# Where the weights' low words are shifted, and for how long TensorE's pauses are filled

## The chip, the cores and the metric

The kernel runs on 1 core of one Trainium2 chip. Times are device microseconds (us); the figure for a kernel is the median of several runs. The engines: TensorE (PE) multiplies, from weights that it loads first (PEld), into PSUM, eight banks of 128 x 2 KB; VectorE (DVE) and ScalarE (ACT) read and write PSUM and SBUF; GpSimd (POOL) works on SBUF alone; SyncE (SP) issues the transfers. Each runs its own queue in order.

## The reference, cut to what matters

Attention, then two mixtures, over 4 x 576 = 2304 tokens of 512 features. q, k and v are float32; the first mixture's and the second's weights are float64, which the kernel receives as pairs of 32-bit words and has to turn into float32 itself.

```python
# attention, 8 heads of 64: pooled by 4 and repeated, plus a band of +-3
out_up = np.repeat(sm_attn(q_d, k_d, v_d), 4, axis=2)
scores = np.where(mask, scale * q @ k.T, -1e9)      # |i - j| < 4
x = out_up + softmax(scores) @ v
# first mixture: 512 -> 2048 -> 512
h = x @ w_in; x = (h * np.cos(h)) @ w_out
# second mixture: 512 -> 1536 -> 512
xn = x / rms * rms_g
out = (silu(xn @ w_gate) * (xn @ w_val)) @ w_out2
```

## The kernel before

Every large product is made of three float32r products (high x high, high x low, low x high). The first mixture goes in units: a `unit` makes a 128 x 512 block of h in one PSUM bank (`h`, L1004), ScalarE, VectorE and again ScalarE and VectorE turn it into h cos h (L1022 to L1029), it is split into high and low (L1038, L1040), and `second` multiplies it with w_out into the banks `y` (L1070). The first tokens' units start while the attention of the other three batches is still to be done; its blocks (`block`: transposes `btr`, scores `bs`, softmax L693 to L706, transposes `bat`, values `bav`) and its pooled part (`pq_part`, `pooled`: `trq`, `sps`, `tra`, `avp`) lie between the units. The second mixture (`gvp` L1493, `o` L1746) comes after, with Strassen-like sums.

The order of all engines' queues comes from a planner, the class `Order`. Every piece of work is a generator that yields its next step, as an engine with a price in us, or a list of alternatives. `start` works out for each when it could begin: the engine's clock `free`, and the end of the step before plus a handover (0.12 on the same engine, 0.3 between engines, 0.2 behind TensorE). Of alternatives it takes the one that ends first, with a handicap as a fifth entry. `run` always takes the step that can start first, ties and near ties by due times. The instructions are issued in that order; on the chip semaphores hold them, not the planner's times. Banks are handed out from a pool in planned time (`take("bank")`).

The conversion of a piece of weights, 128 x 512 float64 words, is `w_conv` (first mixture, 32 pieces) and `w2_conv` (second, 36 pieces, whose result goes back to DRAM). The float64 lies as pairs of int32, low word `lw` and high word `hw`. Its steps: the low word is shifted right by 29 on VectorE (L311, L1295); ScalarE scales the high word, read as float32, by a power of two (L315, L1297); VectorE joins `hw` shifted left by 3 with `lw` (L317, L1299). In the first mixture ScalarE then rounds to float32r (L319) and GpSimd or VectorE takes the difference (L322). The step `yield "ACT", 0.0` ahead of the shift makes it wait, in planned time, for ScalarE's turn.

`keep_warm` (L239) is called whenever TensorE gets a step, with the planned end of its last step and the planned start of this one. Up to the planner's `FT` = 90 it fills `FR` = 0.8 of the pause with float32 products of the 128 x 128 identity, reckoned at 0.22 us each, into a bank that is free at the pause's start (L246). They add nothing to the planner's clocks.

Of the kernel before, what the change touches and what calls it, by code (L numbers as in the profile page):

```python
# [9 lines left out]
F32 = mybir.dt.float32  # L10
F32R = mybir.dt.float32r
I32 = mybir.dt.int32
ACTF = mybir.ActivationFunctionType
ALU = mybir.AluOpType
AX = mybir.AxisListType
# [23 lines left out]
NCV = 5  # L39
FR = 0.8  # L40
FT = 90
SLACK = 2.5
CU = 4
DS = 0
# [2 lines left out]
TP = 5  # L47
WD = 0.005
NQS = 1
CVB, GLB = 9, 0.5  # L50
T0, T1, U1, U2 = 70, 52, 6.5, 4.26
DU = {"conv": 20, "pool": -320, "blk": -200}
# [2 lines left out]
class Order:  # L55
# [102 lines left out]
    def run(self):  # L158
        while self.parts:
            can = [(c, p) for p in self.parts for c in (self.start(p),) if c]  # L160
            assert can, [(p["gen"].__name__, p["req"]) for p in self.parts]
            (t, step), p = min(can, key=lambda x: x[0][0])
            kind = step[1] if step else p["req"][1]

            (t, step), p = min((x for x in can if x[0][0] <= t + self.NEAR and (x[0][1][1] if x[0][1] else x[1]["req"][1]) == kind),
                               key=lambda x: ((x[1]["due"] + (TP if TP and x[0][1] and x[0][1][4] else 0)) * WD + x[0][0], x[0][0]))
            r = p["req"]
            if step is None:
                val = None
                if t > p["t"]:  # L170
                    p["t"], p["eng"] = t, "?"
                if r[0] == "take":
                    have = self.pools[self.which(r)]
                    x = min(have, key=lambda x: x[0])
                    have.remove(x)
                    val = x[1]
            else:
                t, eng, dur, tab, sw = step
                if sw and TP is not None:
                    t += self.TABLE  # L180
                if tab:
                    self.table = tab
                if eng == "PE" and self.fill:
                    self.fill(self.free.get(eng, 0.0), t)
                self.free[eng] = t + dur
                p["t"], p["eng"] = t + dur, eng
                val = (t + dur, eng)
            self.next(p, val)
# [3 lines left out]
def fused_kernel(ctx: ExitStack, tc, q, k, v, w_in, w_out, w_gate, w_val, w_out2, rms_g, mask, bmask, out):  # L192
    nc = tc.nc
    PE, ACT, DVE, POOL, SP = nc.tensor, nc.scalar, nc.vector, nc.gpsimd, nc.sync
    S_ = Order()
# [27 lines left out]
    def bank_tile(i, shape, name):  # L223
        return psum.tile(shape, F32, tag=f"b{i}", name=name)


    ident = const.tile([128, 128], F32, name="ident")
# [7 lines left out]
    ident_r = const.tile([128, 128], F32R, name="ident_r")  # L235
    ACT.activation(out=ident_r, in_=ident, func=ACTF.Copy)

    def keep_warm(t0, t1):

        n = int((t1 - max(t0, 2.5)) * FR / 0.22)  # L240
        have = [x for x in S_.pools["bank"] if x[0] <= t0]
        if t0 > FT or n < 1 or not have:
            return
        t = bank_tile(have[0][1], [128, 128], "warm")
        for _ in range(n):
            PE.matmul(t, ident, ident, start=True, stop=True)  # L246

    S_.fill = keep_warm if FR else None
    ysc = dram.tile([NTILE, 2, 128, DM], F32, name="ysc")
# [44 lines left out]
    def conv_due(m, i):  # L294
        if m == 1:
            return T0 + (i // 4) * CU + (0.0, 5.0)[i % 2] + DU["conv"]
        return T0 + T1 * NTILE + (i // 3) * U2 + (0.0, 0.0, 4.0)[i % 3] + DU["conv"]

    def w_conv(m, i, raw, rp, r):
        if i:  # L300
            yield wait(("cv", m, i - 1))
        cv = yield take("cv")
        p = yield take("wa" if i < NF else "wb" if i < NF + NB else "wa" if i < 32 - NW else "wg")
        done(("cv", m, i), 0.0)
        w = p[1] if p[2] == "wg" else p[0].tile([128, 2, 512], F32R, tag=p[1], name="w" + p[1])
        raw = raw.rearrange("p (b c) -> p b c", c=2)
        hw, lw = raw[:, :, 1], raw[:, :, 0]
        c = hw.bitcast(F32)
        yield "ACT", 0.0
        a = yield "DVE", 0.34  # L310
        DVE.tensor_scalar(out=lw, in0=lw, scalar1=29, scalar2=None, op0=ALU.logical_shift_right)  # L311


        yield "ACT", 0.62
        ACT.activation(out=c, in_=c, func=ACTF.Prelu, scale=2.0 ** -112, alpha=-2.0 ** 32)  # L315
        yield "DVE", 0.7
        DVE.scalar_tensor_tensor(out=hw, in0=hw, scalar=3, in1=lw, op0=ALU.logical_shift_left, op1=ALU.bitwise_or)  # L317
        yield "ACT", 0.62
        ACT.activation(out=w[:, 0], in_=c, func=ACTF.Copy)  # L319
        give("cv", cv)  # L320
        _, e = yield [("POOL", 1.5), ("DVE", 0.8, None, None, CVB)]
        (POOL if e == "POOL" else DVE).tensor_tensor(out=w[:, 1], in0=c, in1=w[:, 0], op=ALU.subtract)  # L322
        give(rp[2], rp)
        give("raw", r)
        W[m, i], WP[m, i] = (w[:, 0], w[:, 1]), p
        done(("w", m, i))
# [298 lines left out]
    def block(b, u, raw, pools):  # L625

        i0, n, r0, off = geo(u)
# [7 lines left out]
        for w in range(2):  # L635
            yield take("att")
            i = yield take("bank")
            t = bank_tile(i, [128, 4, 128], "btr")
# [8 lines left out]
            _, e = yield [("ACT", 0.6), ("DVE", 0.68, None, None, 0.3)]  # L647
# [22 lines left out]
        held = []  # L670
        for e in range(2):
            yield take("att", 1 - e)
            i = yield take("bank")
            held.append((i, bank_tile(i, [128, 4, 64], "bs")))
        yield "PE", 1.0

        for _, t in held:
# [12 lines left out]
        t0 = (S_.cur["t"], "PE")  # L690
# [44 lines left out]
        for e in range(2):  # L735
            yield take("att", 1 - e)
            i = yield take("bank")
            held.append((i, bank_tile(i, [128, 4, 116], "bav")))
        yield "PE", 1.0
        v_i = VI[b, u]  # L740
        for a in range(4):
# [242 lines left out]
    def unit(n):  # L984
# [11 lines left out]
        h = bank_tile(i, [128, 512], "h")  # L996
        for ci, c in enumerate(cs):
            wh, wl = W[1, 2 * c]
            yield "PE", 1.44 if len(cs) > 1 else 2.76
            m = 0  # L1000
            for kk in range(4):
                ksl = slice(kk * 128, kk * 128 + 128)
                for a, x in ((wh, xh), (wh, xl), (wl, xh)):
                    PE.matmul(h[:, w_ * ci:w_ * ci + w_], a[:, ksl], x_at(x, kk), start=m == 0, stop=m == 11)  # L1004
                    m += 1
            if j == len(T1S) - 1:
                free_w(WP[1, 2 * c])
# [280 lines left out]
    def w2_conv(i, raw, p, r):  # L1288
        c, kind = divmod(i, 3)
        pairs = raw.rearrange("p (b c) -> p b c", c=2)  # L1290
        hw, lw = pairs[:, :, 1], pairs[:, :, 0]
        f = hw.bitcast(F32)
        yield "ACT", 0.0
        yield "DVE", 0.34
        DVE.tensor_scalar(out=lw, in0=lw, scalar1=29, scalar2=None, op0=ALU.logical_shift_right)  # L1295
        yield "ACT", 0.62
        ACT.activation(out=f, in_=f, func=ACTF.Prelu, scale=2.0 ** -112, alpha=-2.0 ** 32)  # L1297
        yield "DVE", 0.7
        DVE.scalar_tensor_tensor(out=raw[:, 0:512], in0=hw, scalar=3, in1=lw, op0=ALU.logical_shift_left, op1=ALU.bitwise_or)  # L1299
        yield "SP", 0.8  # L1300
        SP.dma_start(wfs[c, :, 512 * kind:512 * kind + 512], raw[:, 0:512].bitcast(F32))
        give(p[2], p, S_.now())
        give("raw", r, S_.now())
        count(("wfs", c), 3)
# [534 lines left out]
```

## Time and profile before

| | |
|---|---|
| median of 3 runs | 984.79 us (983.96 to 986.35) |
| profiled execution | 986.51 us |
| its span, first to last instruction | 984.7 us |
| mean granted TensorE clock | 0.994 |
| busy: TensorE, VectorE, ScalarE, GpSimd | 97%, 74%, 55%, 27% of the span |

The profile is of one execution. Busy shares are averages over stages with quite different limits; the tables by stage give busy time per engine in a stretch of the span, counted from its start. The granted clock (PEclk) is a share of full speed: 1.00 is 2.4 GHz, 0.50 is 1.2 GHz, and a value between is a stretch with both. In a timeline, the bracket at the end of a row is how long the engine was idle before it, and what ended that. A float32 filler product leaves two matmul records.

### The profile page before, as it was taken

What the parts mean: (1) busy time and instruction counts of PE and PEld (TensorE: products, weight loads), DVE (VectorE), ACT (ScalarE), POOL (GpSimd) and SP (SyncE); (2) the same over time, 40 slices, a digit from 0 to 9 for tenths busy, and PEclk for the clock granted to TensorE, in tenths of its full rate; (3) what the DMA queues carried; (4) which work ended last, traced back from release to release, by engine and by line L of the source; (5) the groups of instructions that cost most, each with busy time, mean ns of one, the idle gap of its engine ahead of it and who ended that gap; (6) DMA issues with size and microseconds to landing.
All of it is one profiled execution on the core that took longest, in us unless ns stands there. A gap on an engine that the chain in (4) does not pass through costs nothing.

```text
span 984.7 us, 19115 instructions
## 1 busy us (share of the span) xinstructions
PE 954.6 (97%) x7102; PEld 881.4 (90%) x7102; DVE 724.0 (74%) x1460; ACT 542.8 (55%) x1090; POOL 268.5 (27%) x325
## 2 busy tenths in 40 slices
PE   7788899999999999999999999999999999999998
PEld 7787788888988888888888889999999999999998
DVE  3889976577767675666577599586666688999895
ACT  3657886577676964657566475242322334544442
POOL 3867675444345311000042252000000014300000
PEclk9999999899999999999999999999999999999999
DMA  8788633567675554544331311133222144454432
GB/s 245 211 234 252 179 116 118 140 204 185 201 220 153 173 168 137 167 153 165 124 129 65 107 43 49 49 105 93 75 81 70 57 146 131 137 169 137 143 119 76
DMA packets 160333, 136.07 MB, mean 138 GB/s; under 512 B 72176, under 2 KB 133744, under 8 KB 160240
## 3 DMA queue, kind: packets, MB, share of 16 engines
q1 hardware_dynamic: 160240, 134.85, 45.4%
q8 instruction: 56, 0.92, 0.4%
q14 instruction: 37, 0.30, 0.1%
HBM read 98.64 MB, written 36.18 MB: 137 GB/s over the span
## 4 chain that ended last, share of the span: by engine, by line
PE 83%; POOL 4%; DVE 3%; SPq 3%; issue 3%; DMA 2%; ACT 2%; DVEq 0%; POOLq 0%; ACTq 0%
PE gvp L1493 26%; PE y L1070 19%; PE h L1004 18%; PE o L1746 13%; PE bav L745 2%; PE btr L641 1%; SPq L475 1%; POOL wwa L322 1%; DMA v<-in_v 1%; SPq L807 1%; PE avp L589 1%; PE bs L684 1%; PE yt L1398 1%; PE bat L720 1%; SPq L478 1%
## 5 line engine op out<-in xcount | busy, mean ns | idle before, releaser
L1493 PE MATMUL gvp<-xc,wc 128*128 128x384 f32 x1296 | 231.7, 335 | 0.0
L1493 PEld LDWEIGHTS gvp<-xc,wc 128*128 128x128 f32 x1296 | 225.6, 188 | 0.3
L1564 DVE TENSOR_TENSOR tmp<-gvp,tmp 128x384 f32<-128x384 f32 x180 | 99.3, 553 | 54.6 <-PE gvp L1493 51.4
L1004 PE MATMUL h<-big,wwa 128*128 128x256 f32 (+1 forms) x756 | 126.1, 320 | 1.6 <-DVE t L1029 1.0
L1004 PEld LDWEIGHTS h<-big,wwa 128*128 128x128 f32 x756 | 109.4, 193 | 11.9 <-DVE t L1029 1.2
L1746 PE MATMUL o<-wo,wc 128*128 128x256 f32 x972 | 118.9, 280 | 0.0
L1746 PEld LDWEIGHTS o<-wo,wc 128*128 128x128 f32 x972 | 116.1, 190 | 0.0
L1070 PE MATMUL y<-wwa,big 128*128 128x512 f32 x432 | 109.6, 398 | 1.7 <-DVE big L1040 1.7
L1070 PEld LDWEIGHTS y<-wwa,big 128*128 128x128 f32 x432 | 78.9, 188 | 18.7 <-DVE big L1040 2.7
L1004 PE MATMUL h<-big,wwb 128*128 128x256 f32 (+1 forms) x504 | 85.2, 320 | 0.1
L1070 PE MATMUL y<-wwb,big 128*128 128x512 f32 x324 | 82.3, 399 | 2.3 <-POOL big L1040 2.3
L1024 DVE SCALAR_TENSOR_TENSOR t<-kk,h 128x512 f32<-128x512 int32 x72 | 49.0, 681 | 42.4 <-ACT kk L1022 42.1
L1004 PEld LDWEIGHTS h<-big,wwb 128*128 128x128 f32 x504 | 73.1, 193 | 7.7 <-issue 0.8
L1022 ACT ACTIVATE kk<-h 128x512 int32<-128x512 f32 x72 | 42.7, 593 | 58.4 <-PE h L1004 58.2
L1070 PEld LDWEIGHTS y<-wwb,big 128*128 128x128 f32 x324 | 59.0, 188 | 14.7 <-POOL big L1040 2.9
L1630 POOL TENSOR_TENSOR wt<-wo 128x256 f32<-128x256 f32 x10 | 9.9, 987 | 208.7 <-DVE wc L1349 183.3
L1029 DVE TENSOR_TENSOR t<-h,t 128x512 f32<-128x512 f32 x72 | 49.3, 685 | 18.1 <-ACT t L1027 17.6
L1555 ACT ACTIVATE tmp<-gvp 128x384 f32<-128x384 f32 x36 | 17.7, 492 | 75.9 <-PE gvp L1493 75.9
L1027 ACT ACTIVATE t<-t,cst 128x512 f32<-128x512 f32 x72 | 51.9, 722 | 13.2 <-DVE t L1024 12.7
L1038 ACT ACTIVATE big<-t 128x512 fp32r<-128x512 f32 x72 | 45.2, 629 | 25.0 <-DVE t L1029 23.6
L1689 ACT ACTIVATE wc<-ut 128x512 fp32r<-128x512 f32 (+1 forms) x60 | 34.3, 584 | 43.4 <-DVE ut L1675 27.2
L1040 DVE TENSOR_TENSOR big<-t,big 128x512 fp32r<-128x512 f32 x54 | 40.0, 741 | 16.5 <-ACT big L1038 16.2
(185 smaller groups left out, 1737.8 us busy)
## 6 DMA issues: line engine op xcount, KB each, us to landing
us<-tmp SPq DMA_DIRECT2D x72, 192.0 KB, 2.0
uf<-us SPq DMA_DIRECT2D x48, 256.0 KB, 2.9
rawwa<-in_moe_w_out SPq DMA_DIRECT2D x21, 512.0 KB, 4.5
wfs<-rawwa SPq DMA_DIRECT2D x36, 256.0 KB, 2.3
rawwa<-in_moe_w_gate SPq DMA_DIRECT2D x12, 512.0 KB, 4.0
rawwa<-in_moe_w_val SPq DMA_DIRECT2D x12, 512.0 KB, 4.4
wf<-wfs SPq DMA_DIRECT2D x12, 512.0 KB, 4.1
vb<-in_v SPq DMA_DIRECT2D x80, 64.0 KB, 2.7
```

Of the source, the lines that this page charges most:

```text
L1004: PE.matmul(h[:, w_ * ci:w_ * ci + w_], a[:, ksl], x_at(x, kk), start=m == 0, stop=m == 11)
L1022: ACT.activation(out=kk, in_=h, func=ACTF.Copy, scale=INV2PI, bias=0.25)
L1024: DVE.scalar_tensor_tensor(out=t, in0=kk, scalar=TWOPI, in1=h, op0=ALU.mult, op1=ALU.subtract)
L1027: ACT.activation(out=t, in_=t, func=ACTF.Sin, scale=-1.0, bias=cst[:, 0:1])
L1029: DVE.tensor_tensor(out=t, in0=h, in1=t, op=ALU.mult)
L1038: ACT.activation(out=gh, in_=t, func=ACTF.Copy)
L1040: (POOL if e == "POOL" else DVE).tensor_tensor(out=gl, in0=t, in1=gh, op=ALU.subtract)
L1070: PE.matmul(y[j][b], g[:, tsl], a, start=(first and ci == 0 and i == 0), stop=(last and c == 15 and i == 2))
L1493: PE.matmul(bank, w[:, a, kk], xc[:, x, b, kk], start=first and i == 0, stop=i == 5, skip_group_check=True)
L1564: DVE.tensor_tensor(out=half(o), in0=a, in1=half(b), op=ALU.add)
L1689: ACT.activation(out=o[:, 0], in_=src, func=ACTF.Copy)
L1746: PE.matmul(b[m][1][:, l], u[0][x][:, j, l], w[:, y, k], start=(p == 0 and l == 0 and i == 0), stop=(p == C3 - 1 and i == 2), skip_group_c ...
```

## The change

The shift becomes a helper, `shift`, used by both conversions. It offers the step to VectorE and to ScalarE, each for 0.6 us (VectorE's price was 0.34), with a handicap `SHB` of 0 for ScalarE. On VectorE the instruction is the old one. On ScalarE an activation reads the upper 16 bits of the low word as unsigned 16-bit integers (every fourth of them), multiplies by 2^-13, adds 2^-14 - 0.5 and writes the result, rounded to an integer, over the low word.

`keep_warm` fills on beyond the planner's 90, until `FT2` = 215: there only pauses of 0.8 us and over, and 0.6 of them. If no bank is free at the pause's start, the products go into a bank that the waiting step itself holds and is about to overwrite, where the step has named one (`own`). The band's scores, the band's values and the units' h do.

```diff
+FT2, FR2 = 215, 0.6
+SHB = 0.0
...
-                    self.fill(self.free.get(eng, 0.0), t)
+                    self.fill(self.free.get(eng, 0.0), t, p)
...
-    def keep_warm(t0, t1):
-        n = int((t1 - max(t0, 2.5)) * FR / 0.22)
+    def keep_warm(t0, t1, p):
+        own = p.pop("own", None)
+        n = int((t1 - max(t0, 2.5)) * (FR if t0 < FT else FR2) / 0.22)
         have = [x for x in S_.pools["bank"] if x[0] <= t0]
-        if t0 > FT or n < 1 or not have:
+        if n < 1 or t0 > FT2 or t0 > FT and t1 - t0 < 0.8:
             return
-        t = bank_tile(have[0][1], [128, 128], "warm")
+        if have:
+            own = bank_tile(have[0][1], [128, 128], "warm")
+        elif t0 < FT or own is None:
+            return
         for _ in range(n):
-            PE.matmul(t, ident, ident, start=True, stop=True)
+            PE.matmul(own, ident, ident[:, :own.shape[-1]], start=True, stop=True, skip_group_check=True)
...
+    def shift(raw, lw):
+        _, e = yield [("DVE", 0.6), ("ACT", 0.6, None, None, SHB)]
+        if e == "ACT":
+            top = raw.bitcast(U16).rearrange("p (b c) -> p b c", c=4)[:, :, 1]
+            ACT.activation(out=lw, in_=top, func=ACTF.Copy, scale=2.0 ** -13, bias=2.0 ** -14 - 0.5)
+        else:
+            DVE.tensor_scalar(out=lw, in0=lw, scalar1=29, scalar2=None, op0=ALU.logical_shift_right)
...
         yield "ACT", 0.0
-        a = yield "DVE", 0.34
-        DVE.tensor_scalar(out=lw, in0=lw, scalar1=29, scalar2=None, op0=ALU.logical_shift_right)
+        yield from shift(raw2, lw)
         yield "ACT", 0.62
...
+        S_.cur["own"] = held[0][1][:, 0:2].rearrange("p a k -> p (a k)")
         yield "PE", 1.0
...
+        S_.cur["own"] = held[0][1][:, 0]
         yield "PE", 1.0
...
+            if ci == 0:
+                S_.cur["own"] = h[:, 0:128]
             yield "PE", 1.44 if len(cs) > 1 else 2.76
```

## Rows read from the trace of the kernel before

**Rows 1.** The page: busy time by engine (part 1); a group of instructions (part 5).

```profile
PE 954.6 (97%) x7102; PEld 881.4 (90%) x7102; DVE 724.0 (74%) x1460; ACT 542.8 (55%) x1090; POOL 268.5 (27%) x325
...
L1022 ACT ACTIVATE kk<-h 128x512 int32<-128x512 f32 x72 | 42.7, 593 | 58.4 <-PE h L1004 58.2
```

**Rows 2.** Busy us by stretch: length, PE, PEld, DVE, ACT, POOL, PEclk, DMA, GB/s.

```profile
70.00:130.00 60.00, 53.92 (x456) 46.63 (x455) 56.90 (x95) 49.48 (x95) 40.75 (x43) 0.97 0.71 204
100.00:160.00 60.00, 55.24 (x431) 48.30 (x430) 50.92 (x99) 51.87 (x105) 42.34 (x49) 0.97 0.48 142
20.00:200.00 180.00, 160.00 (x1557) 142.36 (x1557) 140.70 (x260) 128.00 (x272) 119.60 (x142) 0.97 0.64 182
70.00:200.00 130.00, 119.73 (x1012) 105.59 (x1011) 99.84 (x175) 95.98 (x183) 80.89 (x91) 0.96 0.57 165
200.00:450.00 250.00, 248.34 (x2168) 216.87 (x2167) 170.55 (x331) 169.37 (x315) 74.06 (x100) 1.00 0.60 177
```

**Rows 3.** TensorE's timeline: start, us, instruction, count [idle before <- what ended it].

```profile
96.40 1.42 PE L1070 MATMUL y<-wwa,big 128*128 128x512 f32 x5 [1.17 <-DVE big L1040]
...
106.16 1.54 PE L534 MATMUL sps<-pqs 64*72 64x144 f32 x8 [2.66 <-DVE bst L704]
...
138.12 1.43 PE L1070 MATMUL y<-wwb,big 128*128 128x512 f32 x5 [1.09 <-POOL big L1040]
...
169.28 0.32 PE L745 MATMUL bav<-bt,vb 64*64 64x58 f32 x2 [0.15 <-ACT pqs L396]
171.25 1.96 PE L745 MATMUL bav<-bt,vb 64*64 64x58 f32 x30 [1.64 <-DVE bt L755]
...
187.29 3.14 PE L1004 MATMUL h<-big,wwa 128*128 128x256 f32 x24 [1.01 <-DVE t L1029]
```

**Rows 4.** Busy time by stretch, around the two stretches of lowered clock.

```profile
100.00:110.00 10.00, 7.34 (x50) 6.68 (x49) 9.90 (x19) 9.23 (x14) 5.64 (x7) 0.83 0.87 247
106.00:110.00 4.00, 3.84 (x20) 3.44 (x21) 4.00 (x9) 3.93 (x6) 1.75 (x3) 0.57 0.81 224
170.00:178.00 8.00, 6.75 (x53) 6.62 (x54) 3.80 (x6) 2.85 (x6) 6.79 (x10) 0.57 0.50 107
```

**Rows 5.** Busy time by stretch of L311 alone, the first mixture's shift.

```profile
20.00:200.00 180.00, 21.84 (x32) 0.97 0.64 182
70.00:130.00 60.00, 11.80 (x15) 0.97 0.71 204
100.00:160.00 60.00, 7.73 (x12) 0.97 0.48 142
```

**Rows 6.** Line L311: ns min/median/max, first and last start.

```profile
L311 DVE TENSOR_SCALAR rawwa<-rawwa x18: 376/594/1210, 83.3 to 180.5; 128x512 int32<-128x512 int32 x18
L311 DVE TENSOR_SCALAR rawwb<-rawwb x14: 379/426/1544, 30.7 to 85.3; 128x512 int32<-128x512 int32 x14
```

**Rows 7.** Line L315, the scaling of the high word: ns min/median/max.

```profile
L315 ACT ACTIVATE rawwb<-rawwb x14: 659/676/744, 28.7 to 86.0; 128x512 f32<-128x512 f32 x14
```

**Rows 8.** ScalarE's timeline, 95 to 105 us.

```profile
97.88 1.24 ACT L315 ACTIVATE rawwa<-rawwa 128x512 f32<-128x512 f32 x2
```

**Rows 9.** VectorE's timeline, 96 to 107 us.

```profile
97.46 1.20 DVE L311 TENSOR_SCALAR rawwa<-rawwa 128x512 int32<-128x512 int32 x1
...
99.25 0.88 DVE L311 TENSOR_SCALAR rawwa<-rawwa 128x512 int32<-128x512 int32 x1
...
103.67 1.02 DVE L311 TENSOR_SCALAR rawwa<-rawwa 128x512 int32<-128x512 int32 x1
104.62 1.26 DVE L703 TENSOR_SCALAR bst<-bst 128x8 f32<-128x8 f32 x1
105.91 0.20 DVE L704 RECIPROCAL bst<-bst 128x8 f32<-128x8 f32 x1
```

**Rows 10.** Busy time by stretch of L1295 alone, the second mixture's shift.

```profile
190.00:450.00 260.00, 18.14 (x36) 1.00 0.59 175
```

**Rows 11.** The chain that ended last, 70 to 80 us: start, us, what.

```profile
76.44 0.89 PE warm L246 x8
...
77.48 1.66 PE h L1004 x12
```

More of the change, by code (lines that the diff above doesn't have):

```diff
@@ L12 @@
 I32 = mybir.dt.int32
+U16 = mybir.dt.uint16
 ACTF = mybir.ActivationFunctionType
@@ L305, in w_conv @@
         w = p[1] if p[2] == "wg" else p[0].tile([128, 2, 512], F32R, tag=p[1], name="w" + p[1])
+        raw2 = raw
         raw = raw.rearrange("p (b c) -> p b c", c=2)
@@ L1293, in w2_conv @@
         yield "ACT", 0.0
-        yield "DVE", 0.34
-        DVE.tensor_scalar(out=lw, in0=lw, scalar1=29, scalar2=None, op0=ALU.logical_shift_right)
+        yield from shift(raw, lw)
         yield "ACT", 0.62
```

## The prediction

> **What bounds the kernel now.** I read the page's first part, then a table of busy time by stage, then TensorE's timeline for its waits, and last the stretches in which the clock is low. TensorE is busy 97% of the span [rows 1]. From 200 us on there is nothing to win: in 200 to 450 it is busy 248.34 of 250 us at granted clock 1.00 [rows 2]. What can move lies ahead of that. Between 70 and 200 us TensorE is idle 130 - 119.73 = 10.3 us [rows 2]. Five waits of over a microsecond make 1.17 + 2.66 + 1.09 + 1.64 + 1.01 = 7.6 us of it [rows 3]; VectorE ends four of them, 6.5 us, and GpSimd the one of 1.09.
>
> The clock falls behind two of these waits. Behind the one of 2.66 us it is granted at 0.57 over 4 us, behind the one of 1.64 us at 0.57 over 8 us [rows 4]. At the half level (1.2 instead of 2.4 GHz) a microsecond does half a microsecond's work, so 0.57 leaves 0.43 of the stretch undone: 4 x 0.43 = 1.7 us and 8 x 0.43 = 3.4 us, together 5.1 us. What can be won at all is thus 10.3 + 5.1 = 15.4 us, 1.6%.
>
> Of the helpers VectorE is the fullest first: 56.90 of 60 us in 70 to 130, ScalarE 49.48. In 100 to 160 they stand level, 50.92 and 51.87 [rows 2]. So ScalarE has far less room there than its 55% on the page [rows 1] suggests.
>
> **The change part by part.**
>
> *The shift leaves VectorE.* The first mixture has 32 conversions, and their shifts on VectorE take 21.84 us [rows 5], 0.68 each, from 0.38 to 1.54 [rows 6]. On ScalarE no row shows this operation. The nearest is the step behind it, which also reads and writes every second word of 128x512: 0.66 to 0.74 us [rows 7], and two in a row 1.24 [rows 8], so about 0.6 of the engine's time each. The lower bound is the 0.59 of the activation that writes int32, which reads PSUM [rows 1]; above, I allow for twice the row, 1.35, since the source is now every fourth 16-bit word. I take 0.6, by the neighbour step, which has the same partitions, count and output stride.
>
> How many move: both candidates bid 0.6 with no handicap, and the step is reached when ScalarE's turn comes (the step of zero length ahead of it). From there the planner lets ScalarE start 0.12 later and VectorE 0.3 later, so ScalarE wins unless its queue is over 0.18 us longer. I take about two thirds, 22 of 32 (bounds 10 and 32). In 20 to 200 us VectorE then loses 22 x 0.68 = 15 us and ScalarE gains 22 x 0.6 = 13 us: 140.70 becomes about 126, and 128.00 about 141, of 180 us [rows 2]. The sum hardly changes. But in 70 to 130, where VectorE is full, 15 shifts take 11.80 us [rows 5], and two thirds of these are 8 us of 60.
>
> What of it is on the path: ahead of the longest wait VectorE carries shifts of 1.20, 0.88 and 1.02 us in 97 to 105 us, and then a tiny operation of 1.26 us [rows 9]; the reciprocal behind it ends TensorE's wait of 2.66 us [rows 3]. Taking two of three shifts out gives back 2 us on VectorE, but ScalarE is itself busy 9.23 of 10 us there [rows 4] and takes 1.2 more, so about 0.8 is left for sure. Of the 6.5 us that VectorE ends I count a good third as won, 2.5 us (bounds: -1 if ScalarE hands everything back, 6.5 if all four go). Before 70 us I add 0.5 for shifts standing between steps of the attention blocks (bounds 0 and 2). What is late next is the ScalarE step between two products, the sines and exponentials.
>
> *Second mixture, 36 conversions.* Their shifts take 18.14 us on VectorE [rows 10]. TensorE idles 1.7 us in 200 to 450 [rows 2], so its queued products hide the move: cost and gain 0. If that cover were gone, 24 shifts more on ScalarE, 14 us over the 169.37 of 250 [rows 2], would have to stand in line with its part of a unit, a microsecond or two in all; at 73% it keeps room.
>
> *The planner's other choices.* VectorE's price for a shift goes from 0.34 to 0.6, and every later choice is made against new engine clocks. The order of all work up to 200 us will differ, and the weights' loads on SP's queue with it, since their buffers come free at other times. I price this at 0, with bounds of -3 and +3 us, the size of the longest wait [rows 3].
>
> *The fillers.* They add no planned time. Eight records take 0.89 us on the chain [rows 11], 0.11 each; a product leaves two, so 0.22. They now also go into foreseen pauses of 0.8 us and over until the planner's 215, for 0.6 of the pause, and where no bank is free into the bank that the waiting step itself holds. The waits of that size in the trace sum to 7.6 us, so some 4.5 us of filler, about 20 products, if the plan sees the same ones. They can give back the 5.1 us of clock. The part of 3.4 us stands well: two banks are waited for one after the other, the first one's products have started (two records at 169.28, then 1.64 us of wait [rows 3]), so fillers into the first bank run in that wait. The other wait is for a step that has no bank of its own to offer. I take half, 2.5 us (bounds 0 and 5.1).
>
> What they cost: a filler ahead of a step that is ready earlier than planned delays it, since the queue runs in order. In the kernel before, 0.89 us of filler lie on the chain that sets the end [rows 11]. A filler into the very bank that is waited for starts only when the step itself could have started, and is paid in full. A quarter of 4.5 us gives 1.1 us of loss (bounds 0 and 4.5).
>
> **Sum.** -2.5 - 0.5 + 0 + 0 - 2.5 + 1.1 = -4.4 us. The profiled execution took 986.51 us (span 984.7, 1.8 around it), so it would take 982.1. The median of the runs shown, 984.79, is 1.72 below the profiled one, which gives **980.4 us**. Differences under 0.3%, 3 us, are what a measurement here cannot tell from none.
>
> **The rivals.**
>
> A. *ScalarE becomes the bound; slower.* In 100 to 160 us ScalarE is busy 51.87 of 60 us [rows 2]. If all 12 shifts of that stretch [rows 5] go there, 12 x 0.6 = 7.2 us fill 8.1 us of slack, and each conversion has two steps in a row on the engine for which sines and exponentials wait. It decides once ScalarE is above some 95%, which is from 9 of the 12 on (51.87 + 5.4 = 57.3). If half the added time comes out at TensorE, +3.6 us, and new waits bring as much lowered clock as now, the median is 988.4. For it: the bid favours ScalarE. Against: the same planner sees ScalarE's queue and can give VectorE the copies that either engine may do. The Trainium skill, in "ScalarE: Activation LUTs", section "Rules for kernel authors", wants simple arithmetic on VectorE rather than ScalarE. For one shift by itself the trace agrees, 0.38 undisturbed against 0.66 at least; by that rule the change would lose, and rival A's time is where.
>
> B. *Nothing to be measured.* The waits are ended by something else next, the pauses that drop the clock are not the foreseen ones, or gains and fillers cancel: 982 to 987.7. It includes the case that the choice leaves most shifts on VectorE.
>
> C. *Nearly all is won.* Both losses of clock (5.1) and 5 of the 6.5 us of VectorE's waits, with 1 us of filler: -9.1, 975.7. Against: a plan made anew has waits of its own.
>
> **How the numbers follow.** Forecast, 977 to 982: 0.46. C: 0.11. B: 0.20. A: 0.23. So faster 0.57, within 0.3% 0.20, slower 0.23. The range from 974.0 to 989.0 takes in A and C and leaves some 2 in 10 beyond it: the terms' bounds reach further, to about -17 and +10, but not together. The likeliest case by itself is 977 to 982.
>
> **What would show it.** Right: ScalarE has a line for the shift, with about 22 of the first 32 at 0.6 to 0.7 us; VectorE in 70 to 130 falls from 57 to about 50 us; no stretch of 6 us at the half clock between 100 and 200 us; filler records until some 200 us; TensorE's idle time in 70 to 200 falls from 10.3 to about 7 us. Wrong: ScalarE above 95% in 100 to 160 with TensorE's waits ended by it; fillers on the chain of waits; lowered clock elsewhere; a shift of over 1 us on ScalarE; or any difference that arises after 200 us.

## The result: 0.7% slower, and the profile after

| | median of 6 | range |
|---|---|---|
| before | 985.19 us | 983.96 to 986.35 |
| changed | 992.61 us | 988.86 to 994.53 |

The ratio is 1.0069 [1.0053, 1.0085]: slower by 7.4 us, where 4.4 us faster was forecast. The profiled execution of the changed kernel is the shortest of its six (988.86 us, span 987.1, mean granted clock 0.997; the other five have spans of 987.6 to 992.7 and clocks of 0.990 to 0.995). So the profile shows only 987.1 - 984.7 = 2.4 us of the loss.

The page after: busy time (part 1), then the chain's shares (part 4) by engine and by line. The second fence is the chain's shares before.

```profile
PE 953.4 (97%) x7112; PEld 877.9 (89%) x7112; DVE 705.3 (71%) x1403; ACT 567.1 (57%) x1142; POOL 269.5 (27%) x328
...
PE 68%; DVE 8%; DMA 8%; ACT 8%; issue 4%; POOL 2%; SPq 1%; DVEq 0%; ACTq 0%; POOLq 0%
PE gvp L1510 26%; PE o L1763 13%; PE y L1088 12%; PE h L1022 11%; DMA wfs<-rawwa 2%; DMA rawwa<-in_moe_w_gate 2%; PE bav L761 1%; DMA rawwa<-in_moe_w_val 1%; DMA rawwa<-in_moe_w_out 1%; ACT t L1045 1%; SPq L823 1%; DVE rawwb L331 1%; ACT L1045 1%; ACT rawwa L311 1%; PE warm L253 1%
```

```profile
PE 83%; POOL 4%; DVE 3%; SPq 3%; issue 3%; DMA 2%; ACT 2%; DVEq 0%; POOLq 0%; ACTq 0%
```

VectorE has lost 18.7 us of work and ScalarE gained 24.3 [rows 1], as meant. What is new is in the chain: it ran 2% over transfers, now it runs 8%, some 79 us, and the transfers named are the loads of the float64 weights (`rawwa`) and the stores of the converted ones (`wfs`).

Busy time by stage, columns as in [rows 2]; the last two are stretches of lowered clock.

```profile
0.00:70.00 70.00, 54.92 (x630) 50.44 (x631) 40.71 (x79) 41.53 (x111) 44.30 (x65) 0.95 0.82 223
70.00:130.00 60.00, 53.93 (x480) 47.93 (x479) 50.84 (x78) 52.79 (x95) 42.65 (x42) 1.00 0.74 212
100.00:160.00 60.00, 53.57 (x413) 46.18 (x412) 44.83 (x80) 56.27 (x103) 40.07 (x42) 1.00 0.52 148
70.00:200.00 130.00, 122.30 (x1038) 107.81 (x1036) 92.72 (x150) 108.18 (x203) 86.55 (x96) 1.00 0.59 167
200.00:450.00 250.00, 244.83 (x2169) 212.09 (x2169) 162.51 (x307) 174.91 (x338) 71.92 (x101) 1.00 0.62 182
450.00:580.00 130.00, 129.05 (x598) 107.06 (x597) 92.11 (x193) 82.28 (x165) 32.32 (x35) 1.00 0.26 93
...
10.00:20.00 10.00, 6.99 (x47) 6.72 (x47) 2.49 (x2) 2.22 (x6) 4.91 (x8) 0.83 0.93 287
60.00:70.00 10.00, 7.56 (x100) 7.02 (x101) 7.80 (x17) 5.94 (x13) 6.38 (x7) 0.83 0.71 227
```

The kernel before, the two stretches that [rows 2] leave out:

```profile
0.00:70.00 70.00, 56.55 (x654) 52.18 (x655) 45.29 (x89) 37.48 (x102) 46.31 (x67) 1.00 0.83 231
450.00:580.00 130.00, 130.00 (x604) 108.13 (x603) 93.80 (x196) 81.58 (x165) 34.17 (x36) 1.00 0.28 99
```

What TensorE loses in a stage is its idle time and the clock not granted, (1 - PEclk) x length:

| stage | before | after | difference |
|---|---|---|---|
| 0 to 70 us | 13.4 + 0 | 15.1 + 3.5 | +5.1 |
| 70 to 200 | 10.3 + 5.2 | 7.7 + 0 | -7.8 |
| 200 to 450 | 1.7 + 0 | 5.2 + 0 | +3.5 |
| 450 to 580 | 0 | 0.95 | +0.95 |

The sum is +1.75, and 5 more fillers (117 products against 112, 0.22 each) add 1.1: 2.85 us. The granted clock is printed to 0.01, so a row of 130 us can be off by 0.65. The second mixture's first product (`gvp`) starts 2.7 us later than before, 579.6 instead of 576.9, and from there on both kernels take the same time.

Fillers count as busy time, and they stand elsewhere now: ahead of 70 us there are 101 products instead of 108, behind it 16 instead of 4. TensorE's timeline behind 70 us has one row of them before, and after it has these three and the six products shown further below:

```profile
76.27 1.06 PE L246 MATMUL warm<-ident 128*128 128x128 f32 x8
```

```profile
77.69 1.06 PE L253 MATMUL warm<-ident 128*128 128x128 f32 x8
89.92 1.16 PE L253 MATMUL warm<-ident 128*128 128x128 f32 x8
101.81 0.61 PE L253 MATMUL warm<-ident 128*128 128x128 f32 x4
```

The 12 more at 0.22 us make 2.6 us, which is all by which the idle time of 70 to 200 fell. So the waits there did not get shorter on balance, they were filled; what the stage gained is 5.2 us of clock. That was lost again ahead of it, and behind it in the stage where I had expected nothing.

The shift after, by line (ns min/median/max, first and last start):

```profile
L311 ACT ACTIVATE rawwa<-rawwa x42: 647/676/727, 86.8 to 427.4; 128x512 int32<-128x512 uint16 x42
L311 ACT ACTIVATE rawwb<-rawwb x11: 651/678/746, 30.5 to 81.3; 128x512 int32<-128x512 uint16 x11
L313 DVE TENSOR_SCALAR rawwa<-rawwa x12: 414/830/1544, 94.3 to 357.1; 128x512 int32<-128x512 int32 x12
```

53 of the 68 shifts went to ScalarE: 21 of the first mixture's 32, and 32 of the second's 36. What they wait for is seen in ScalarE's waits (line, what it waited for: us in total, times, longest), after, 185 to 450 us:

```profile
ACT rawwa L311 <- DMA rawwa<-in_moe_w_val: 14.1, 6, 4.1
ACT rawwa L311 <- DMA rawwa<-in_moe_w_gate: 12.6, 6, 3.4
...
ACT rawwa L311 <- DMA rawwa<-in_moe_w_out: 1.8, 2, 1.1
ACT rawwa L311 <- DMA v<-in_v: 1.7, 1, 1.7
```

and the same view of the kernel before:

```profile
ACT rawwa L1297 <- DMA rawwa<-in_moe_w_out: 7.4, 3, 3.6
```

ScalarE stands 14.1 + 12.6 + 1.8 + 1.7 = 30.2 us at shifts whose data has not landed; before, it stands 7.4 us at the scaling, then its first step of a conversion. VectorE's own waits for these loads are 1.1 us after and 5.4 before, so the two engines together have 31.3 against 12.8. The loads land some 4 us after they are issued, hardly later than before (4.0 and 4.4); the planner counts a step of 1.5 us on SyncE and 2.0 behind it. The DMA issues of the page after (KB each, median us to landing):

```profile
rawwa<-in_moe_w_gate SPq DMA_DIRECT2D x12, 512.0 KB, 4.3
rawwa<-in_moe_w_val SPq DMA_DIRECT2D x12, 512.0 KB, 4.6
```

The Trainium skill, in "DMA: Bandwidth & Descriptors", section "Anatomy of one DMA — SWDGE (gpsimd) path", gives a fixed 2.0 us and a part that grows with the bytes (divided by 436e3); for 512 KB that makes an estimate of 3.2 us. It is fitted for another issuing path than SyncE's. The trace has 4.3 and 4.6 beside other transfers, and the measurement decides; the planner's 3.5 in all lies under both.

One such wait, ScalarE's timeline and then TensorE's, after:

```profile
293.87 0.68 ACT L311 ACTIVATE rawwa<-rawwa 128x512 int32<-128x512 uint16 x1 [2.33 <-DMA rawwa<-in_moe_w_val]
294.56 1.28 ACT L714 ACT_TABLE_LOAD   x1
295.86 0.63 ACT L714 ACTIVATE bt<-bt 128x512 f32<-128x512 f32 x1
296.39 0.61 ACT L1056 ACTIVATE big<-t 128x512 fp32r<-128x512 f32 x1
```

```profile
297.06 0.49 PE L1088 MATMUL y<-wwa,big 128*128 128x512 f32 x1 [0.59 <-ACT big L1056]
```

The exponential, with 1.28 us for its table, and the unit's rounding (`big`) stand behind the shift in ScalarE's queue, and TensorE's product behind the rounding. This place costs TensorE 0.59 of its 5.2 us; its longest waits in 200 to 450 are 1.2 us for a copy on VectorE and 1.1 for one on ScalarE, and these were not followed back to a load one by one.

### The profile page after: what moved, and what is told of

Read it like the earlier page. It is cut to its first block, busy times and chain, and to the rows that moved or that the text cites. A ratio compares the mean times of both kernels' runs of the same rounds, so it can differ in the third digit from the quotient of the medians.

```text
span 987.1 us, 19119 instructions
## 1 busy us (share of the span) xinstructions
PE 953.4 (97%) x7112; PEld 877.9 (89%) x7112; DVE 705.3 (71%) x1403; ACT 567.1 (57%) x1142; POOL 269.5 (27%) x328
## 4 chain that ended last, share of the span: by engine, by line
PE 68%; DVE 8%; DMA 8%; ACT 8%; issue 4%; POOL 2%; SPq 1%; DVEq 0%; ACTq 0%; POOLq 0%
PE gvp L1510 26%; PE o L1763 13%; PE y L1088 12%; PE h L1022 11%; DMA wfs<-rawwa 2%; DMA rawwa<-in_moe_w_gate 2%; PE bav L761 1%; DMA rawwa<-in_moe_w_val 1%; DMA rawwa<-in_moe_w_out 1%; ACT t L1045 1%; SPq L823 1%; DVE rawwb L331 1%; ACT L1045 1%; ACT rawwa L311 1%; PE warm L253 1%
## 5 line engine op out<-in xcount | busy, mean ns | idle before, releaser
L1022 PE MATMUL h<-big,wwb 128*128 128x256 f32 (+1 forms) x504 | 82.6, 317 | 0.0
L1088 PEld LDWEIGHTS y<-wwb,big 128*128 128x128 f32 x324 | 59.0, 188 | 11.9 <-DVE big L1058 0.3
L1045 ACT ACTIVATE t<-t,cst 128x512 f32<-128x512 f32 x72 | 51.4, 721 | 12.6 <-DVE t L1042 12.2
L1058 POOL TENSOR_TENSOR big<-t,big 128x512 fp32r<-128x512 f32 x17 | 22.8, 1342 | 110.0 <-ACT big L1056 92.0
```

The lines of the kernel that those rows point to most:

```text
L1045: ACT.activation(out=t, in_=t, func=ACTF.Sin, scale=-1.0, bias=cst[:, 0:1])
L1058: (POOL if e == "POOL" else DVE).tensor_tensor(out=gl, in0=t, in1=gh, op=ALU.subtract)
L1088: PE.matmul(y[j][b], g[:, tsl], a, start=(first and ci == 0 and i == 0), stop=(last and c == 15 and i == 2))
```

## The experiments

Each was timed in five rounds beside the kernel before (its medians 983.9 to 985.0 on the chips used). Where a diff is against another experiment, the text says so.

### The two parts of the change, each alone

Only the planner's choice, no longer filling:

```diff
-FT2, FR2 = 215, 0.6
+FT2, FR2 = FT, 0.6
```

> The changed kernel without the longer filling: same planner's order, but 8 products of filler fewer (2, and 6 into h's own bank, at 101.8 and 105.2 us of the changed kernel's trace). Theory W (waits): the changed kernel is slow because the shift is the first reader of freshly loaded weights and now stands in ScalarE's queue, where it waits for the transfer (31.6 us in 18 waits in the changed kernel, against 8.4 us in 4 waits of ScalarE before) with sines and evictions behind it; then this kernel is about as slow as the changed one, 990 to 994. Theory F (fillers): the 6 products into the bank that h waited for cost 1.3 us and lead to more; then this kernel is near the kernel before, 984 to 988. Theory R (re-planning): any new order moves the time by a few us either way; then it is as slow as the changed one too.

997.60 us, 1.0115 [1.0085, 1.0146], above the 990 to 994 expected; in its profiled execution, the slowest of six, TensorE is idle 10.4 us in 200 to 450. Only the longer filling, with the shift back on VectorE at 0.34 in both conversions, so that all engines' order is the old one:

```diff
-        yield from shift(raw2, lw)
+        yield "DVE", 0.34
+        DVE.tensor_scalar(out=lw, in0=lw, scalar1=29, scalar2=None, op0=ALU.logical_shift_right)
```

> The kernel before with the longer filling alone: shift on VectorE at its old price, the same order, 24 products more (5.3 us of filler), among them 3 and 5 into the bank of bav at the wait of 1.64 us behind which the clock was lowered. By the prediction's term: 3.4 us of lowered clock come back there and about 1 us of filler is paid, 981.5 to 984. Theory F: fillers are paid, 986 to 989. Theories W and R say nothing against the prediction's term here: this part is then worth its -1 to -3.5 us and the loss is all the shift's.

983.94 us, 0.9995 [0.9982, 1.0007]. So the choice is what loses. The filling does what was forecast of it in one place. The stretch of [rows 4] whose clock was 0.57, with filling alone, and TensorE's timeline in it:

```profile
170.00:178.00 8.00, 7.74 (x107) 7.28 (x106) 4.28 (x7) 4.47 (x10) 7.48 (x9) 1.00 0.43 105
```

```profile
171.14 1.37 PE L253 MATMUL bav<-ident 128*128 128x116 f32 x10
```

Five products into the bank that the values wait for hold the clock at 1.00. Yet 24 products more (136 against 112) bring nothing that can be measured. In the changed kernel's order 8 products more, at 101.8 and 105.2 us, go with 997.60 - 992.61 = 5 us. Where these arise was not found: the two intervals touch at 1.0085, and the kernel without them ran in anything from 990.87 to 1000.77 us.

### The choice in one conversion alone

The first mixture only (no longer filling, and `w2_conv` back on VectorE), and the second only (`w_conv` back):

```diff
 def w2_conv
-        yield from shift(raw, lw)
+        yield "DVE", 0.34
+        DVE.tensor_scalar(out=lw, in0=lw, scalar1=29, scalar2=None, op0=ALU.logical_shift_right)
```

> The shift's choice of engine in the first mixture's conversions alone (32), the second's on VectorE at 0.34, no longer filling. Theory W: the loads of the first mixture are waited for only 5 times or so on ScalarE, so within 2 us of the kernel before, 983 to 987. Rival A of the prediction (ScalarE is full at 100 to 160 us): slower, 987 to 990. Theory R: anything from 981 to 990, with a start of the h products that differs by about 1 us.

> The choice in the second mixture's conversions alone (36), the first's on VectorE at 0.34, no longer filling. Theory W: ScalarE waits some 20 us or more for the transfers of in_moe_w_gate, in_moe_w_val and in_moe_w_out between 190 and 430 us, TensorE's idle time in 200 to 450 rises from 1.7 to 4 to 6 us, and the kernel is slower, 988 to 993, with runs farther apart than those of the kernel before (2.4 us). The prediction's term (0): 984 to 986.5. Rival A: 985 too.

First alone 990.71 us, 1.0055 [1.0033, 1.0076]; second alone 997.11 us, 1.0124 [1.0105, 1.0143]. Each loses by itself, and the second, priced at 0, loses most. Both lie above what theory W expected (983 to 987 and 988 to 993), and they do not add up: 0.55% and 1.24% alone, 1.15% together. TensorE's row with the second alone:

```profile
200.00:450.00 250.00, 242.97 (x2107) 210.51 (x2099) 156.46 (x297) 178.74 (x334) 77.19 (x105) 0.99 0.59 170
```

It is idle 7.0 us there instead of 1.7, and ScalarE waits 25.5 us for loads. One chain of cause and effect, in the timelines of ScalarE, VectorE and TensorE of that kernel:

```profile
280.58 0.65 ACT L311 ACTIVATE rawwa<-rawwa 128x512 int32<-128x512 uint16 x1 [4.96 <-DMA vb<-in_v]
281.14 0.82 ACT L411 ACTIVATE pqs<-trq 64x256 f32<-64x256 f32 x2
281.98 0.60 ACT L665 ACTIVATE bt<-btr 128x512 f32<-128x512 f32 x1
282.48 0.71 ACT L1046 ACTIVATE t<-t,cst 128x512 f32<-128x512 f32 x1
```

```profile
283.22 0.69 DVE L1048 TENSOR_TENSOR t<-h,t 128x512 f32<-128x512 f32 x1 [5.14 <-ACT t L1046]
```

```profile
282.01 2.93 PE L1023 MATMUL h<-big,wwa 128*128 128x256 f32 x12 [3.21 <-ACT pqs L411]
```

The shift waits 4.96 us for transfers. Behind it stand an eviction (`pqs`), a copy and a unit's sine, and TensorE waits 3.21 us for the eviction. The product that then starts takes 2.93 us where its like at 285.32 takes 1.68, since the clock has fallen:

```profile
282.00:286.00 4.00, 3.99 (x22) 3.99 (x23) 1.52 (x3) 3.97 (x6) 0.00 (x0) 0.60 0.51 149
```

### The engine, or the order?

The order kept as it was, and only the instruction put on ScalarE: the second mixture's 36 shifts (the diff, against the kernel before), and the first's 32 in the same way. Theory L in the first text is that ScalarE simply has too much to do.

```diff
         yield "DVE", 0.34
-        DVE.tensor_scalar(out=lw, in0=lw, scalar1=29, scalar2=None, op0=ALU.logical_shift_right)
+        top = raw.bitcast(U16).rearrange("p (b c) -> p b c", c=4)[:, :, 1]
+        ACT.activation(out=lw, in_=top, func=ACTF.Copy, scale=2.0 ** -13, bias=2.0 ** -14 - 0.5)
```

> The kernel before with its planned order on every engine kept, but the second mixture's 36 shifts are issued on ScalarE at the place where VectorE's stood. ScalarE gets 24 us more, VectorE 18 us less, and TensorE's, GpSimd's and SyncE's queues are the same. Theory L: slower by 5 us or more, 990 to 997. Theory W: ScalarE's first look at each load comes 0.6 us earlier than before, but from an order in which the loads mostly lie ready; its waits for transfers rise from 8 to 10 to 18 us and the time by 1 to 4 us, 985.5 to 989. Theory R: as the kernel before, 984 to 986.

> The kernel before with its planned order on every engine, but the first mixture's 32 shifts are issued on ScalarE in VectorE's place; TensorE's, GpSimd's and SyncE's queues stay. Rival A of the prediction (ScalarE is full at 100 to 160 us): ScalarE rises there from 52 to about 58 of 60 us and the time by 3 us or more, 988 to 992. The prediction's term for VectorE's relief: -1 to -3 us, 982 to 984. Theory W: as the kernel before or up to 2 us slower, since few of these loads are waited for, 984 to 987.

984.66 us, 0.9999 [0.9991, 1.0007], and 983.78 us, 1.0005 [0.9995, 1.0015]: nothing. For the second's shifts theory W had 985.5 to 989, a miss: in the old order the two engines' waits for these loads do not rise (9.3 us, 12.8 before). Rows of the two, one stretch each:

```profile
200.00:450.00 250.00, 249.51 (x2170) 217.84 (x2164) 156.52 (x297) 187.10 (x352) 71.15 (x100) 1.00 0.61 179
```

```profile
100.00:160.00 60.00, 54.10 (x428) 46.66 (x427) 47.99 (x84) 57.14 (x117) 39.36 (x49) 1.00 0.51 143
```

ScalarE has more to do than in the changed kernel (187.10 against 174.91, and 57.14 against 56.27), and TensorE is idle 0.5 us in 200 to 450. What loses is not work on ScalarE. Nor does VectorE's relief win: with all 32 of the first mixture's shifts off it, TensorE is idle 130 - 119.18 = 10.8 us in 70 to 200, 10.3 before. The product that waited 2.66 us for VectorE [rows 3] now waits for ScalarE (TensorE's waits in that kernel):

```profile
PE sps L537 <- ACT pqs L399: 3.2, 1, 3.2
```

The other way round, the order of the kernel with the choice in the second conversion, but each shift issued on VectorE:

```diff
 def shift
         if e == "ACT":
-            top = raw.bitcast(U16).rearrange("p (b c) -> p b c", c=4)[:, :, 1]
-            ACT.activation(out=lw, in_=top, func=ACTF.Copy, scale=2.0 ** -13, bias=2.0 ** -14 - 0.5)
+            DVE.tensor_scalar(out=lw, in0=lw, scalar1=29, scalar2=None, op0=ALU.logical_shift_right)
```

> The order of the kernel with the choice in the second mixture alone (997.1 us), on every engine, but the shifts planned for ScalarE are issued on VectorE in the same place. If the order is what costs and not the engine, as in the two kernels that kept the old order and moved the shifts the other way without a difference: 993 to 999. If ScalarE's standing in line at the shift is the cost: VectorE waits instead, ScalarE only at the next step, 0.6 us later, and the time falls by 3 us or more, 986 to 994.

993.67 us, 1.0091 [1.0076, 1.0106]: most of the 1.0124 stays, and both engines now stand for loads. The time lies in both expected ranges: about three quarters of the loss come with the order, and 997.11 - 993.67 = 3.4 us go when the shift leaves ScalarE's queue. ScalarE's waits in that kernel, 185 to 450 us:

```profile
ACT rawwa L1314 <- DMA rawwa<-in_moe_w_gate: 9.4, 5, 2.6
...
ACT rawwa L1314 <- DMA rawwa<-in_moe_w_out: 9.1, 5, 2.8
...
ACT rawwa L1314 <- DMA rawwa<-in_moe_w_val: 3.3, 3, 1.7
```

That is 21.8 us on ScalarE, whose first step of a conversion is now the scaling, and 25.3 us on VectorE in the same stretch (5.4 before). So most of the loss is in the order, which brings a conversion to its engine ahead of its load.

### Is any new order worse?

The old kernel with another price for the shift on VectorE, all shifts staying there, which gives a new order each time:

```diff
-        yield "DVE", 0.34
+        yield "DVE", 0.6
```

> The kernel before with VectorE's price of both shifts at 0.6 instead of 0.34, all on VectorE, no longer filling: a new order and nothing else. Theory R: 3 to 10 us away from the kernel before, as far as the other new orders. Theories W and L: within 3 us, 982 to 988, since no wait moves to ScalarE.

> A second new order with all shifts on VectorE, whose price is 0.45 in both conversions instead of 0.34 (0.6 gave 1.0009 of the kernel before). Theory R (any new order loses some 0.5% against this one): 988 to 994. If it is the choice of ScalarE that makes the orders bad: 982 to 988.

At 0.6: 985.59 us, 1.0009 [0.9996, 1.0023]. At 0.45: 983.27 us, 0.9985 [0.9972, 0.9997]. A plan made anew need not cost anything. Nor does the sum of the waits for loads set the time: at 0.6 ScalarE and VectorE stand 10.4 and 11.9 us for the second mixture's loads, 12.8 together before, and TensorE's idle time in 200 to 450 is 1.4 us. What stands behind such a wait must decide; that was not measured by itself.

### The loads landing earlier, against the order

If the order loses by loads not landed, loads that land sooner in the same order must give it back. The second mixture's loads and conversions were cut to 32 of the 128 partitions (128 KB instead of 512; the stored weights repeat these rows four times), in three kernels: the choice in the second conversion alone, the kernel before as control, and the changed kernel.

```diff
-                SP.dma_start(raw, s32)
+                SP.dma_start(raw[0:32], s32[0:32])
...
 def w2_conv
+        raw = raw[0:32]
...
-        SP.dma_start(wfs[c, :, 512 * kind:512 * kind + 512], raw[:, 0:512].bitcast(F32))
+        SP.dma_start(wfs[c, :, 512 * kind:512 * kind + 512].rearrange("(r p) f -> p r f", p=32), raw[:, 0:512].bitcast(F32).unsqueeze(1).to_broadcast([32, 4, 512]))
```

> The same order, shifts on ScalarE, but the second mixture's loads and conversions use 32 of the 128 partitions (a quarter of the bytes; the instructions take the same time; the converted words of 32 partitions are stored four times over, so the second mixture's weights are not the reference's). The loads land earlier, nothing else changes in any queue. Theory W: ScalarE's waits for them fall from 25 us to under 10 and the time by half the loss or more, 985 to 991. Theory R (the order is bad in other ways): 993 to 998.

> The control for it: the kernel before with the same smaller loads and conversions on 32 partitions. Its waits for these loads are 7.4 us on ScalarE and 5.4 on VectorE already, and TensorE idles 1.7 us in that stretch: within 2 us of the kernel before, 982 to 986.

> The changed kernel itself, its order and fillers kept, with the second mixture's loads and conversions on 32 of 128 partitions (stored four times over, so its weights are not the reference's); in the old order this changed nothing (1.0003). Theory W for the changed kernel: ScalarE's 30 us of waits for these loads fall under 10, and of its loss of 0.69% the larger part goes, 984 to 988. If the first mixture's new order carries the loss: 989 to 993.

| order of | full loads | small loads |
|---|---|---|
| choice in the second alone | 1.0124 [1.0105, 1.0143] | 1.0047 [1.0033, 1.0060] |
| before | 1 | 1.0003 [0.9993, 1.0013] |
| changed | 1.0069 [1.0053, 1.0085] | 1.0005 [0.9993, 1.0018] |

In the changed kernel the whole loss goes (985.12 us), and nothing goes in the old order, so small loads are no gain in themselves. Its stage row, its loads and its waits, the changed kernel with small loads:

```profile
200.00:450.00 250.00, 248.07 (x2198) 216.14 (x2197) 164.37 (x309) 177.72 (x344) 72.94 (x105) 1.00 0.51 132
```

```profile
rawwa<-in_moe_w_gate SPq DMA_DIRECT2D x12, 128.0 KB, 3.0
```

```profile
ACT rawwa L311 <- DMA rawwa<-in_moe_w_gate: 5.8, 3, 2.9
ACT rawwa L311 <- DMA rawwa<-in_moe_w_val: 4.3, 3, 2.1
...
ACT rawwa L311 <- DMA v<-in_v: 1.1, 1, 1.1
```

Landing 1.3 us sooner (1.8 for `in_moe_w_val`, 4.6 to 2.8) takes the waits from 30.2 to 11.2 us and TensorE's idle time in the stage from 5.2 to 1.9. The order and ScalarE's instructions are those of the changed kernel, some of them on fewer partitions, at 177.72 us of work. The stage also moves less (132 GB/s against 182), so other transfers have less beside them too; that was not told apart.

### Planning with a later landing

The planner told that a load lands 3 us later: for the second conversion (against the kernel with the choice there alone), for both (against the changed kernel), and for the first (against the choice there alone).

```diff
-            S_.add(w2_conv(i, raw, p, r), due2(0), S_.now())
+            S_.add(w2_conv(i, raw, p, r), due2(0), S_.now() + LAND)
```

> The kernel with the choice in the second mixture alone (997.1 us), but the planner counts the 36 loads' landing 3 us later, so that it queues the conversions behind work that is ready. ScalarE's load is the same. Theory W (ScalarE stands in line for transfers that land later than planned): ScalarE's waits for transfers fall from 28 us to under 8, and most of the loss of 12.4 us goes, 984 to 989. Theory L (ScalarE simply has too much to do from 190 to 430 us): 994 to 998. Theory R (each new order has its own luck): anything from 983 to 997, with waits of no one kind.

> The changed kernel whole, with the planner counting every weights' load, of the first and the second mixture, as landing 3 us later. Theory W (ScalarE waits for transfers that land later than planned): its waits for them fall from 32 us to under 10, and with them most of the changed kernel's loss, 983 to 988. Theory R (a new order has its own luck): anywhere from 984 to 994, and no closer tie to those waits.

> The kernel with the choice in the first mixture alone (990.7 us), with the first mixture's loads counted as landing 3 us later. Theory W, if it holds for this part too: 984 to 988. If the part's loss has another cause (its order leads to waits of TensorE at 62 and 106 us for evictions by VectorE and ScalarE, 4.4 and 3.2 us, and to a long wait for a load at 440 us): still 988 to 992.

The second: 988.72 us, 1.0041 [1.0029, 1.0052], so 0.83 of the 1.24% come back; ScalarE waits 3.3 us for loads, and TensorE is idle 2.6 us in 200 to 450. Both: 989.89 us, 1.0066 [1.0054, 1.0078], a miss: the waits fell to 9.3 us, but TensorE is idle 5.8 us in 200 to 450 behind other steps. The first: 997.46 us, 1.0143 [1.0121, 1.0166], a miss to the other side, against 1.0055 without. A later landing in the plan thus helps the second conversion and harms the first; each makes a plan anew, and what the plan loses elsewhere is in these three numbers too.

### A better version

Three kernels: longer filling alone, with the scaling of a gain vector moved behind the work that I took it to hold up (the diff below); that with the second mixture's shifts on ScalarE in the old order besides; and the price of 0.45 with longer filling and the moved scaling.

```diff
-        DVE.tensor_scalar(out=gv_, in0=gv_, scalar1=-0.125, scalar2=None, op0=ALU.mult)
         S_.add(words(32), 0.0)
...
         done("xl")
+        DVE.tensor_scalar(out=gv_, in0=gv_, scalar1=-0.125, scalar2=None, op0=ALU.mult)
```

> The kernel before with the longer filling alone (983.9 us), and the scaling of the four columns of rms_g, which stands in VectorE's queue at 58 us and waits there for its load (0.6 us in the kernel before, 2.0 in the kernel with filling alone, 2.6 with the choice in the first mixture), issued at some 440 us instead, where its first reader is near. Nothing else in any queue changes. If that wait is what moves the start of the h products between 67.5 and 69.6 us and drops the clock at 60 to 70 us: start at 66.5 to 67.5 us, 981 to 983. If the wait is covered by another: as the filling alone, 983 to 985.

> What the runs so far point to: the order of the kernel before, the longer filling, the scaling of rms_g's columns issued late (984.0 us with these two), and the second mixture's shifts issued on ScalarE in VectorE's place (984.7 by itself). If the three add up, 982 to 984; if the shifts' move brings nothing even so, 983.5 to 985.

> The new order with all shifts on VectorE at 0.45 (983.3 us, 0.9985), with the longer filling and the scaling of rms_g's columns issued late, which gave 0.9987 in the old order. If they add up: 981 to 983, 0.997. If filling is worth as little as in the old order (0.9995): 982.5 to 984.

984.03 us, 0.9987 [0.9975, 1.0000]; 983.33 us, 0.9992 [0.9981, 1.0002]; 982.77 us, 0.9982 [0.9965, 0.9999]. The last has the lowest time of the eighteen and is faster than the changed kernel. Against the old one its 0.18% is less than the 0.3% that the prediction takes for no change, and the price of 0.45 by itself has 0.9985. The first was a miss: the first unit's product starts at 68.7 us, where 66.5 to 67.5 was expected.

## Why the prediction was wrong, step by step

**The step that failed** is "*Second mixture, 36 conversions* ... so its queued products hide the move: cost and gain 0", and with it "*The planner's other choices* ... I price this at 0, with bounds of -3 and +3". For the instruction by itself the 0 was right (0.9999 in the old order). The new order was priced at 0 as well, and the kernel lost 7.4 us, beyond the +3 allowed for it. I looked at how full ScalarE was and not at what the shift reads. It is the first step that touches a freshly loaded piece; when it may go to ScalarE, it stands in that queue ahead of sines, evictions and roundings, and in the new order it gets there before the load lands. 30.2 us of such waits, 7.4 before, and TensorE's idle time in 200 to 450 from 1.7 to 5.2 us. Shown by the exchange of order and engine (0.9999 and 1.0005 for the engine alone, 1.0091 for the order with VectorE), and by the loads landing sooner (1.0069 to 1.0005, control 1.0003). The part on the shift named the waits that it takes off VectorE, and none that it brings to ScalarE's queue.

**The rival that I gave for this side, A, falls.** ScalarE's work in 100 to 160 us did reach the point named, 56.27 and with the first mixture's shifts all there 57.14 of 60 us, and that kernel takes 983.78 us, no change, though ScalarE took over the longest wait. The rule weighed there (the Trainium skill, "ScalarE: Activation LUTs", "Rules for kernel authors": simple arithmetic rather on VectorE) has the sign of the result, but not its cause: moved in the old order, the same work costs nothing.

**Shifts off VectorE, -2.5:** right in its counts, and not in its gain. Forecast 22 of the first 32, at 0.6 to 0.7 us: 21, at 0.65 to 0.75. VectorE in 70 to 130 to about 50: 50.84. TensorE's idle time in 70 to 200 to about 7: 7.7, but by luck, since the 2.6 us are the 12 more fillers there. In the old order all 32 shifts off VectorE left 10.8 us idle: ScalarE handed back what VectorE gave, the case that I had put at the lower bound. Of the second's 36 I had 24 moving; 32 did.

**The start, -0.5:** wrong in the profiled execution. 0 to 70 us loses 5.1 us more, 1.6 idle (7 fewer fillers) and 3.5 in two stretches at 0.83, and the first unit's product starts at 69.1 instead of 67.8. Kernels with the old order there start it anywhere from 67.1 to 69.6 in their profiles, so it is not shown that the change delays it.

**Clock, -2.5, and fillers, +1.1:** no stretch of lowered clock is left between 100 and 200 us, so 5.2 us came back there, the higher bound; as much as 3.5 went at the start. For the larger part that is luck. Of some 20 products foreseen behind the planner's 90 us the changed kernel has 8, and none near 170. The kernel with its order and no longer filling has a full clock there too, since TensorE does not wait there in that order; between 100 and 200 us it has lowered clock in one stretch only, where the changed kernel has 1.00. First two rows without the longer filling, then one of the changed kernel:

```profile
110.00:120.00 10.00, 9.41 (x44) 7.82 (x44) 7.98 (x16) 7.89 (x15) 3.56 (x3) 0.83 0.18 44
170.00:180.00 10.00, 10.00 (x78) 9.44 (x76) 5.64 (x11) 7.73 (x16) 4.58 (x7) 1.00 0.34 101
```

```profile
110.00:120.00 10.00, 9.56 (x59) 7.89 (x60) 9.27 (x17) 9.22 (x17) 5.45 (x4) 1.00 0.44 112
```

The filling alone is worth 0.9995, about nothing where -1.4 was forecast. The warning on the own bank was right for the unit. TensorE's timeline after:

```profile
105.25 1.60 PE L253 MATMUL h<-ident 128*128 128x128 f32 x12 [1.96 <-ACT bt L664]
106.61 1.68 PE L1022 MATMUL h<-big,wwa 128*128 128x256 f32 x12
```

Six products, 1.36 us up to the unit's start, run once the bank is ready and put the unit off by as much. Yet they were not lost. Without them the unit starts at 105.46 us, the next product of `y` waits for VectorE's split until 110.59 (110.41 with them), and at the lowered clock its eleven products take 4.37 us, 2.79 with them. The transpose behind them (`trq`) starts at 113.23 us with the six and at 114.79 without, so in these two profiles they win 1.6 us.

**The sign by which I would have seen it** stood there: "any difference that arises after 200 us". It had no price.

**What stays open.** The first mixture's choice alone loses 5.4 us (0.55%); its profile has TensorE idle 4.6 us in 200 to 450 and the clock at 0.99, with 12.1 us of waits for the weights' loads on ScalarE and 8.9 on VectorE, which is the same kind of loss; that it is the same cause was not shown, and the later landing made it worse. Its loads were not tried smaller. In the second's order some 4 us remain when loads land sooner or are planned later (1.0047, 1.0041), though ScalarE's waits for them are down to 5.0 and 3.3 us; that order loses by something else too. And of the 7.4 us the profile holds 2.4; the other executions, with lower mean clocks, have none.

## What to carry to other kernels

The first instruction that reads a transfer holds up its engine's queue until the transfer lands (here up to 4.96 us), so before a planner may place it anew, list what stands behind it there, and price it with the landing time that the trace shows (here 4.3 to 4.6 us, planned as 1.5 and 2.0). When a planner may choose an engine, two things change, the engine and the order of everything: test the instruction on the other engine in the old order, and the new order with the old engine, before giving either the blame. Idle time that fillers cover is not time won, so count their products by stage. A stage with slack in every engine's busy time can still lose, if the slack is not where the queue stands.

## What the runs showed of the hardware

- Reading every fourth 16-bit word and writing every second 32-bit word, the activation takes 0.65 to 0.75 us for 128x512, the same as the step beside it with float32 on both sides (0.66 to 0.74, [rows 7]).
- On a quarter of the partitions it is hardly shorter: 0.65 to 0.68 us for the 30 such shifts in the kernel with the choice in the second alone and small loads. And a quarter of a load's bytes lands only 1.3 to 1.8 us sooner (3.0 against 4.3, 2.8 against 4.6).
